# A streaming-window attention and SwiGLU kernel: sink values of one batch loaded by two POOL loads instead of eight SP loads

## The chip, the cores and the metric

The kernel runs on one core of a Trainium2 chip. Five engines of the core appear: TensorE (PE; its weight loads are PEld), VectorE (DVE), ScalarE (ACT), GpSimd (POOL) and SyncE (SP). SP, ACT and POOL each issue DMA transfers to a queue of their own; those that POOL issues change the type of the data on the way (float32 in memory to bfloat16 on the chip) where the destination asks for it. The metric is device time in microseconds (us), the median of several runs; smaller is better.

## What is computed

The inputs are `q`, `k`, `v` of shape (4, 8, 768, 64) (batch, heads, positions, width of a head) and three weight matrices. The reference, cut to what matters:

```
scores = q @ k^T / sqrt(64)
keep   = (key < 4) or (0 <= query - key < 128)     # 4 "sinks" and a window
x      = softmax(scores where keep) @ v            # heads side by side: (3072, 512)
g      = x @ w_gate                                # 512 -> 1536
out    = (g * sigmoid(g) * (x @ w_val)) @ w_out    # 1536 -> 512
```

Every query sees the keys of its window and, besides, the first four keys of its sequence, the sinks. So the values of `v` at positions 0 to 3 of each head are needed by all later queries of the batch.

## The kernel before

**Tiles and stages.** Attention goes by 12 groups of 256 queries, three to a batch. For a group the kernel brings `k` and `q` into transposed form, multiplies them (`step_S`, L271), takes exponentials on ACT, masks them on DVE (L298; group 0: L602), and multiplies with the values `va` (`step_PV`, L332, matmuls in L349). A group that isn't the first of its batch also takes the sinks: `step_K` (L302) makes their scores from `kss`, and `step_sinks` (L322, matmul L329) puts their share into the sum, from a tile `vsb`. The normed result is transposed (`step_X`) into `xT`. The feed-forward part works on blocks of 256 or 512 tokens: `project` (L408, matmuls L414) for gate (`pg`) and value (`pv`), tanh on ACT, two products on DVE, then `down` (L486). A list written by hand weaves the attention steps of later groups into the feed-forward steps of earlier blocks. The order of each engine's instructions is the order in which the program writes them.

**Sink values.** `vcf` holds the sink values of batch 0 in float32: four rows for each head, heads 0 to 3 in partitions 0 to 15, heads 4 to 7 in partitions 32 to 47, a column of ones beside them, the rest zero (DVE memsets, L162 and L163). `load_sinks(vcf, 0, 1)` (L178 to L184) fills it with eight loads of SP, one for each head, 4 rows of 64 values (1 KB) each. POOL then copies partitions 0 to 63 to 64 to 127 (L196). `step_vsb(0)` (L262, called in L632) multiplies `vcf` with a mask of heads `diag_h` on POOL and gives `vsb`, which the sink matmuls of group 1 read. Batches 1 to 3 have `vcl` in place of `vcf`, filled by the same function later (L644).

**The first loads.** SP and ACT bring the first half of the heads of group 0 (`st`, L175) in float32. POOL's instructions then follow in this order: the other half (`x0`, L186), two iotas, the `rows` of group 1 (L100, four loads), the values `va` of groups 0 and 1 (L122, four loads), the first weight tiles `wg` and `wv` (L133), the copy of `vcf` (L196), two small copies into `kss` (L259), two more pairs of weight tiles, `vsb` (L264), then the `nat` tiles of group 2 (L111) and all later loads. The first feed-forward matmuls of TensorE (`gate_held`, L466) need the first `wg` tile. Behind them in TensorE's order stand the sink matmuls of group 1 and the PV matmuls of group 1.

Of the kernel before, what the change touches and what calls it, by code (L numbers as in the profile page):

```python
# [14 lines left out]
def kernel(  # L15
# [12 lines left out]
    nc = tc.nc  # L28
    P = 128
    B, H, S, D = q.shape  # L30
    NS = int(n_sink)
# [63 lines left out]
    def load_rows(g, i):  # L95
        b, c = divmod(g, GC)
        if g not in rows:
            new_rows(g)
        for w in range(2):
            nc.gpsimd.dma_start(  # L100
                rows[g][64 * w:64 * (w + 1), i],
                by_rows((k, q)[i], b, w, ALL, c * 256))

    def load_nat(g):
        b, c = divmod(g, GC)
        x = (natp if g > 3 else rowp).tile(
            [P, 2, 2, DM], BF16, tag="nat" if g > 3 else "rows", name="nat")
        for i, src in ((0, k), (1, q)):
            for j in range(2):
                t0 = c * 256 + j * P  # L110
                nc.gpsimd.dma_start(  # L111
                    x[:, i, j].rearrange("p (h d) -> p h d", d=D),
                    src[b, :, t0:t0 + P].rearrange("h p d -> p h d"))
        nats[g] = x

    def load_v(g):
        b, c = divmod(g, GC)
        va = vpool.tile([P, 2, H, VS], BF16, tag=f"va{g}", name="va")
        nc.vector.memset(va[:, :, :, D:D + 1], 1.0)
        for j in range(2):  # L120
            t0 = c * 256 + j * P
            nc.gpsimd.dma_start(  # L122
                va[:, j, :, 0:D], v[b, :, t0:t0 + P].rearrange("h p d -> p h d"))
        vas[g] = va
# [3 lines left out]
    def load_gate(i, which=(0, 1)):  # L128
        f0, n = sum(FCH[:i]) * P, FCH[i] * P
        both = (wgs, moe_w_gate, "wg"), (wvs, moe_w_val, "wv")  # L130
        for lst, w, nm in (both[x] for x in which):
            t = wpool.tile([P, DMC, n], BF16, tag=f"{nm}{i}", name=nm)
            nc.gpsimd.dma_start(  # L133
                t, w[:, f0:f0 + n].rearrange("(c p) f -> p c f", p=P))
            lst.append(t)
# [12 lines left out]
    vcf = const.tile([P, 1, D + 1], FP32)  # L148
# [29 lines left out]
    def load_sinks(t, b0, b1):  # L178
        for h in range(H):
            r = 32 * (h // 4) + NS * (h % 4)  # L180
            nc.sync.dma_start(
                t[r:r + NS, :, 0:D], v[b0:b1, h, 0:NS].rearrange("b s d -> s b d"))

    load_sinks(vcf, 0, 1)  # L184
    for i in range(2):
        nc.gpsimd.dma_start(x0[:, i, 4:8], by_two((k, q)[i], 4))  # L186
    nc.gpsimd.iota(tq, [[1, P]], base=0, channel_multiplier=0,
# [3 lines left out]
    load_rows(1, 0)  # L191
    load_rows(1, 1)
    load_v(0)
    load_v(1)
    load_gate(0)
    nc.gpsimd.tensor_copy(out=vcf[64:128], in_=vcf[0:64])  # L196

    nc.vector.tensor_scalar(ident, tq, tk, None, op0=ALU.is_equal)
    tq2 = tq.rearrange("p (o x) -> p o x", o=1).broadcast_to([P, 2, P])
# [62 lines left out]
    def step_vsb(b):  # L262
        vsb = const.tile([P, 4, D + 1], BF16, tag=f"vsb{b}", name="vsb")
        (nc.vector if b else nc.gpsimd).tensor_tensor(  # L264
            vsb,
            (vcl[:, b - 1:b] if b else vcf).broadcast_to([P, 4, D + 1]),
            diag_h.rearrange("q (h o) -> q h o", o=1).broadcast_to([P, 4, D + 1]),
            op=ALU.mult)
        vsbs.append(vsb)
# [359 lines left out]
    step_ks(0)  # L629
    load_gate(1)  # L630
    load_gate(2)
    step_vsb(0)  # L632
    load_nat(2)
    load_gate(3)
# [120 lines left out]
```

## Time and profile before

| what | us |
|---|---|
| median of 3 runs | 237.57 (237.53 to 237.66) |
| the profiled execution, its own time | 238.22 |
| its span, first to last instruction | 236.4 |
| TensorE busy in it | 228.7 |
| VectorE busy | 157.5 |
| ScalarE busy | 113.0 |
| POOL busy | 75.3 |

The granted clock of TensorE was 1.00 throughout. The profile is one execution, so its durations are summed against its own 238.22 us; the median of the unprofiled runs is 0.65 us lower.

How to read the lines. In the chain of work that ended last, a line has the start, the duration and what ran. In the timeline a line has the start, the duration, the engine, the line of the program, the operation, its tiles and shapes, and how many such instructions the line takes together. In the waits, a line names who waited for whom, with the total, the number and the longest wait. In the list of DMA issues the last number is the median time from the start of the issue to the landing. In the busy time by stretches a line has the stretch, its length, the busy time of PE, PEld, DVE, ACT and POOL with the number of instructions, the granted clock, the mean share of the DMA engines with packets in flight (over 1 where packets overlap) and the rate in GB/s.

### The profile page before, as it was taken

The page shows a single profiled execution, that of the slowest core. Times are in us where ns is not written, and L with a number is a line of the kernel's source. Part 1 is how long each engine was busy: PE and PEld are TensorE (multiplying, and loading weights), DVE is VectorE, ACT ScalarE, POOL GpSimd, SP SyncE. Part 2 cuts the span into 40 slices and gives each one's busy share as a digit, 9 for nine tenths or more (in the row PEclk, how much of TensorE's full clock was granted, in tenths as well). Part 3 has the DMA queues.
Part 4 walks back from the last instruction along what each step waited for, and adds up shares of the span by engine and source line. Part 5 has one row for each costly group of instructions (what it writes and reads, how often), then busy time and mean ns, then how long its engine had stood idle before and what let it go on. Part 6 is the DMA issues. An engine that isn't in the chain of part 4 may idle for free.

```text
span 236.4 us, 4873 instructions
## 1 busy us (share of the span) xinstructions
PE 228.7 (97%) x1867; PEld 127.7 (54%) x1893; DVE 157.5 (67%) x333; ACT 113.0 (48%) x230; POOL 75.3 (32%) x102
## 2 busy tenths in 40 slices
PE   8979999999999999999999999999999999999994
PEld 5659645795555644544445444444444445488443
DVE  4898888768650988960888980698970598877000
ACT  4784485467453836412836522655622663333221
POOL 8996875723501409204435350080000000000000
PEclk9999999999999999999999999999999999999999
DMA  7999999995998949997979996599314100200132
GB/s 137 156 191 176 182 199 205 159 145 79 153 225 168 134 72 76 129 134 172 144 114 136 132 140 168 133 87 116 67 24 143 58 3 0 44 3 1 47 132 90
DMA packets 108743, 27.62 MB, mean 117 GB/s; under 512 B 95792, under 2 KB 105776, under 8 KB 108720
## 3 DMA queue, kind: packets, MB, share of 16 engines
q0 software_dynamic: 76640, 13.90, 79.2%
q1 hardware_dynamic: 30672, 11.58, 25.2%
q10 hardware_dynamic: 1408, 1.84, 2.8%
q8 instruction: 15, 0.25, 0.4%
q14 instruction: 8, 0.07, 0.1%
HBM read 28.34 MB, written 6.29 MB: 147 GB/s over the span
## 4 chain that ended last, share of the span: by engine, by line
PE 89%; POOL 3%; DMA 3%; issue 1%; ACT 1%; DVE 1%; POOLq 0%; DVEq 0%; ACTq 0%
PE pv L414 26%; PE pd L499 26%; PE pg L414 26%; PE o L349 4%; PE s L286 4%; DMA wg<-in_moe_w_gate_dram 3%; POOL va L122 1%; POOL rows L100 1%; PE o L329 1%; PE pn L239 1%; POOL x L186 1%; ACT th L434 1%; PE pk L314 1%; PE px L393 0%; DVE u L442 0%
## 5 line engine op out<-in xcount | busy, mean ns | idle before, releaser
L442 DVE SCALAR_TENSOR_TENSOR u<-th,pg 128x512 bf16<-128x512 f32 x72 | 49.2, 683 | 39.4 <-ACT th L434 39.4
L414 PE MATMUL pg<-xT,wg 128*128 128x512 bf16 (+1 forms) x353 | 73.4, 336 | 1.9 <-DMA wg<-in_moe_w_gate_dram 1.2
L434 ACT ACTIVATE th<-pg 128x512 f32<-128x512 f32 x72 | 43.4, 603 | 63.1 <-PE pg L414 57.2
L414 PE MATMUL pv<-xT,wv 128*128 128x512 bf16 (+1 forms) x349 | 72.9, 336 | 0.6 <-ACT e L293 0.2
L499 PE MATMUL pd<-wo,ht 128*128 128x512 bf16 (+2 forms) x292 | 64.5, 371 | 0.5 <-issue 0.2
L414 PEld LDWEIGHTS <-wg 128*128 128x128 bf16 x360 | 35.0, 98 | 29.1 <-DMA wg<-in_moe_w_gate_dram 1.5
L453 DVE TENSOR_TENSOR ht<-u,pv 128x512 bf16<-128x512 bf16 x62 | 42.7, 688 | 9.4 <-PE pv L414 2.5
L293 ACT ACTIVATE e<-s 128x512 bf16<-128x512 f32 (+1 forms) x88 | 42.9, 583 | 3.7 <-PE s L286 3.6
L499 PEld LDWEIGHTS <-ht 128*128 128x128 bf16 x300 | 27.9, 98 | 30.3 <-issue 0.3
L414 PEld LDWEIGHTS <-wv 128*128 128x128 bf16 x360 | 32.1, 98 | 20.3 <-issue 1.7
L504 ACT ACTIVATE ot<-pd 128x512 f32<-128x512 f32 (+1 forms) x24 | 14.3, 596 | 46.7 <-PE pd L499 42.7
L111 POOL DMA_DIRECT2D nat<-in_k_dram x20 | 17.7, 890 | 39.5 <-DMA qT<-nat 35.8
L298 DVE TENSOR_TENSOR e<-e,mask 128x1024 bf16<-128x1024 bf16 (+1 forms) x44 | 27.1, 654 | 3.7 <-ACT e L293 3.7
L122 POOL DMA_DIRECT2D va<-in_v_dram x24 | 21.4, 917 | 4.7 <-DMA wo<-in_moe_w_out_dram 2.5
L363 DVE TENSOR_TENSOR xn<-o,rcp 128x256 bf16<-128x256 f32 x45 | 19.1, 424 | 1.5
L349 PEld LDWEIGHTS <-e 128*128 128x128 bf16 x352 | 15.2, 98 | 7.9 <-issue 0.2
L111 POOL DMA_DIRECT2D nat<-in_q_dram x20 | 17.7, 900 | 1.1 <-DMA wg<-in_moe_w_gate_dram 0.5
L349 PE MATMUL o<-va,e 128*128 128x65 bf16 x352 | 17.2, 194 | 0.1
L286 PE MATMUL s<-qT,kT 64*128 64x128 bf16 (+1 forms) x240 | 13.1, 238 | 0.0
L286 PEld LDWEIGHTS <-kT 64*128 64x128 bf16 x240 | 7.7, 94 | 7.4 <-issue 6.4
L506 DVE TENSOR_SCALAR ot<-pd 128x128 f32<-128x128 f32 x1 | 0.3, 292 | 14.3 <-PE pd L499 14.3
L357 DVE RECIPROCAL rcp<-o 128x4 f32<-128x4 f32 x48 | 8.3, 175 | 1.4 <-PE o L349 1.3
(74 smaller groups left out, 91.5 us busy)
## 6 DMA issues: line engine op xcount, KB each, us to landing
out_dram<-ot SPq DMA_DIRECT2D x17, 256.0 KB
va<-in_v_dram POOLq DMA_DIRECT2D x24, 128.0 KB, 6.2
nat<-in_k_dram POOLq DMA_DIRECT2D x20, 128.0 KB, 4.1
nat<-in_q_dram POOLq DMA_DIRECT2D x20, 128.0 KB, 5.5
wg<-in_moe_w_gate_dram POOLq DMA_DIRECT2D x6, 256.0 KB, 7.9
wv<-in_moe_w_val_dram POOLq DMA_DIRECT2D x6, 256.0 KB, 8.2
wo<-in_moe_w_out_dram POOLq DMA_DIRECT2D x4, 384.0 KB, 11.1
out_dram<-ot ACTq DMA_DIRECT2D x6, 256.0 KB
```

What stands on the lines that cost most here:

```text
L111: nc.gpsimd.dma_start(x[:, i, j].rearrange("p (h d) -> p h d", d=D), src[b, :, t0:t0 + P].rearrange("h p d -> p h d"))
L122: nc.gpsimd.dma_start(va[:, j, :, 0:D], v[b, :, t0:t0 + P].rearrange("h p d -> p h d"))
L286: nc.tensor.matmul(pss[2 * pp + h][:, col:col + n], kTs[b][r, p, kk:kk + P], qTs[b][r, p, qq:qq + n], start=True, stop=True)
L293: nc.scalar.activation(e_t[g][:, h0 + h, lo:512], pss[2 * pp + h][:, lo:512], AF.Exp, scale=scale)
L298: nc.vector.tensor_tensor(e, e, m[:, :, lo:512].broadcast_to([P, 2, 512 - lo]), op=ALU.mult)
L349: nc.tensor.matmul(o, l, r, start=(c == 0 and i == 0), stop=(i == len(mms) - 1), skip_group_check=True)
L363: nc.vector.tensor_tensor(xn, po[:, :, 0:D], rcp.broadcast_to([P, 4, D]), op=ALU.mult)
L414: nc.tensor.matmul(ps[:, i * n:(i + 1) * n], ws[fi][:, c, fo * P:(fo + 1) * P], xTs[tb][:, c], start=(c == 0), stop=(c == DMC - 1))
L434: nc.scalar.activation(th, pg, AF.Tanh, scale=0.5)
L442: nc.vector.scalar_tensor_tensor(u, th, 1.0, pg, op0=ALU.add, op1=ALU.mult)
L453: nc.vector.tensor_tensor(hts[tb][:, f:f + 512 // SIZES[tb]].rearrange("p a n -> p (a n)"), u, pv, op=ALU.mult)
L499: nc.tensor.matmul(po, hts[tb][:, f, ts * P:(ts + 1) * P], wos[f // n][:, f % n, lo:hi], start=(f == 0), stop=(f == DFC - 1))
```

## The change

`load_sinks(vcf, 0, 1)` and its eight SP loads are gone. In their place POOL issues two loads, each of 16 rows of 64 values (four heads at once), between the `va` loads of group 0 and those of group 1. `vcf` is float32, so these two loads don't change the type. The copy of `vcf` into its other half, still on POOL, is moved from behind the first weight tiles to just ahead of `step_vsb(0)`, behind the issues of the second and third pairs of weight tiles.

```diff
-    load_sinks(vcf, 0, 1)
     for i in range(2):
         nc.gpsimd.dma_start(x0[:, i, 4:8], by_two((k, q)[i], 4))
...
     load_v(0)
+    for a in range(2):
+        nc.gpsimd.dma_start(vcf[32 * a:32 * a + 4 * NS, 0, 0:D],
+                            v[0, 4 * a:4 * a + 4, 0:NS])
     load_v(1)
     load_gate(0)
-    nc.gpsimd.tensor_copy(out=vcf[64:128], in_=vcf[0:64])
...
     step_ks(0)
     load_gate(1)
     load_gate(2)
+    nc.gpsimd.tensor_copy(out=vcf[64:128], in_=vcf[0:64])
     step_vsb(0)
     load_nat(2)
```

`load_sinks` stays for `vcl`. In the instruction lists POOL has two loads more, SP eight fewer; the instructions of the other engines and their order are the same.

## The prediction

> **What bounds the kernel now.** I read the page first, then the chain that ended last, then the waits of TensorE. TensorE is busy nearly all of the span, so a change counts only where TensorE stands still.
>
> ```profile
> PE 228.7 (97%) x1867; PEld 127.7 (54%) x1893; DVE 157.5 (67%) x333; ACT 113.0 (48%) x230; POOL 75.3 (32%) x102
> ```
>
> The chain says where the start is late: four steps of POOL issuing loads, then the flight of the first gate weights, then dense matmuls.
>
> ```profile
> 1.24 1.65 POOL x L186 x2
> 3.31 2.41 POOL rows L100 x4
> 5.72 3.43 POOL va L122 x4
> 9.16 6.91 DMA wg<-in_moe_w_gate_dram
> 16.11 1.05 PE pg L414 x8
> ```
>
> The waits of TensorE from 14 to 30 us have one row (total, times, longest):
>
> ```profile
> PE pg L414 <- DMA wg<-in_moe_w_gate_dram: 1.2, 1, 1.2
> ```
>
> So TensorE stands idle until 16.11 us for the first `wg` tile, issued by POOL at 9.16. Later waits are short, so a shift of this landing reaches the end nearly whole. The change puts two loads on POOL ahead of that issue. The question is whether the issue or the queue behind it sets the landing.
>
> The DMA issues, asked in stretches (last column: us from issue to landing), answer it: `va` in 7.4 to 8.6, `wg` in 9.1 to 9.5, and a load of `va`'s bytes and row lengths, `nat`, in 55 to 59, where the casting queue (q0) had been empty:
>
> ```profile
> va<-in_v_dram POOLq DMA_DIRECT2D x3, 128.0 KB, 5.4
> ```
>
> ```profile
> wg<-in_moe_w_gate_dram POOLq DMA_DIRECT2D x1, 256.0 KB, 6.9
> ```
>
> ```profile
> nat<-in_k_dram POOLq DMA_DIRECT2D x2, 128.0 KB, 3.8
> ```
>
> With an empty queue 128 KB land after 3.8 us, here after 5.4: each `va` load stands 5.4 - 3.8 = 1.6 us behind earlier bytes. Successive weight tiles land 1.34 us apart (9.16 + 6.9 = 16.06; the next, issued at 9.90 with 7.5, at 17.4). If the second 128 KB of a tile cost half of that, `wg` alone in the queue would take 3.8 + 0.7 = 4.5; it takes 6.9, so 2.4 us are queue.
>
> The busy time by stretches (last two columns: DMA share, GB/s) agrees. From 10 to 12 us POOL issues without a pause. From 22 to 23 POOL is itself stopped, waiting for landings, so there the queue is surely full, and the rate is the same:
>
> ```profile
> 10.00:11.00 1.00, 1.00 (x37) 0.83 (x33) 0.97 (x3) 1.00 (x4) 0.96 (x3) 1.00 2.26 144
> 11.00:12.00 1.00, 1.00 (x33) 0.85 (x29) 0.99 (x5) 0.80 (x2) 0.92 (x4) 1.00 2.43 155
> ...
> 22.00:23.00 1.00, 1.00 (x11) 0.89 (x10) 0.90 (x3) 0.56 (x1) 0.58 (x1) 1.00 2.40 155
> ```
>
> **The change, part by part.**
>
> *Eight SP loads go.* Their issues take 0.276 us each, from 1.8 to 4.9 us. SP's next instruction waits 36.7 us for a POOL memset, so that time is worth nothing. Their packets share the DMA engines with the first POOL loads: SP's queue shows 2.2, 1.7, 2.7 and 0.8% of 16 engines in the four microseconds from 4 to 8, 7.4% or 1.2 engine-us. Spread over 16 engines this is 0.07 us, all on one engine that everyone waits for 1.2 us. The rate before and after their last packet (143 GB/s in 6 to 7, 155 in 7 to 8) hardly moves. Same rows are loaded in both kernels, so I take 0; ends -1.2 and 0.
>
> *Two loads of 16 rows are issued by POOL* at about 7.4, between the second and third `va`. The trace has no such load. `rows` loads (64 x 4 = 256 rows) go 0.61 us start to start, `va` loads (128 x 8 = 1024 rows) 0.875. A straight line through these gives 0.61 - 0.265 x 240/768 = 0.53 for 16 rows. Ends: 0.25 (the shortest SP issue of these sinks) and 0.875. Two cost 1.06, ends 0.5 and 1.75. Third and fourth `va`, `wg` and `wv` are issued that much later. Hidden: 1.06 is under the 1.6 of the `va` loads and the 2.4 of `wg`. At 1.75 the excess over 1.6, 0.15 us, is late; without that cover the 1.06 is late. Taken: 0.
>
> The Trainium skill, "DMA: Bandwidth & Descriptors", "Issuing engine by pattern", speaks against this: it gives simple loads to SP and calls that path generally faster. The rows agree on the issue (0.276 on SP, 0.61 and more on POOL), yet SP's time is free here and POOL's covered; by the rule alone the change would cost POOL's 1.06 us.
>
> *The copy of `vcf` moves* from 10.79 (0.43 to the next start) to behind the four weight issues. `kss` and what follows move by 1.06 - 0.43 = +0.63: `kss` ends at 12.3, and its reader, the `pk` matmuls, start at 13.43. The copy then starts at 14.63 + 0.63 = 15.26. It now waits for the two loads: they stand between the second `va` (6.54 + 5.4 = 11.9) and the third (12.8), so they have landed 2.4 us earlier. Behind the copy on POOL stand `vsb`, the `nat` loads and later weights. `vsb` (0.62) would end at 15.26 + 0.39 + 0.62 = 16.27; its reader is the first sink matmul, at 17.09, in order behind `pg`. Spare: 0.8 us; with the loads at 1.75 in all, 0.1.
>
> The loads behind come 1.06 later. `nat` lands after 8.5 us where 3.8 is the empty queue's time, so 4.7 us of queue cover it. From 18.98 to 23.52 POOL idles 0.20 + 0.58 + 0.64 + 0.94 = 2.4 us for landings, and the delay is gone there.
>
> *DVE beside the moved copy.* `vsb` stood just ahead of four masks of DVE, and the first mask shows it:
>
> ```profile
> 14.63 0.62 POOL L264 TENSOR_TENSOR vsb<-vcf,diag_h 128x260 bf16<-128x260 f32 x1
> ```
>
> ```profile
> 14.90 0.90 DVE L298 TENSOR_TENSOR e<-e,mask 128x1024 bf16<-128x1024 bf16 x1
> ```
>
> ```profile
> 16.92 0.68 DVE L298 TENSOR_TENSOR e<-e,mask 128x1024 bf16<-128x1024 bf16 x1
> ```
>
> Beside `vsb` a mask takes 0.90, alone 0.68: 0.22 us of contention. Now copy and `vsb` both fall inside the masks (14.9 to 17.6, less 0.2). Ends: 0, and a POOL that gets nothing until the last mask ends at 17.4. I take one rest of a mask for each, 2 x 0.22 = 0.44: `vsb` at 16.7, still 0.4 early.
>
> The Trainium skill, "SBUF — State Buffer", "Who interferes with whom", says that a DVE instruction with two SBUF inputs and a GpSimd one that reads SBUF shut each other out, whichever comes first holding on to its end. The 0.90 fits. By the rule each of the two could wait a whole 0.68 mask: an estimate of 16.27 + 1.36 = 17.6, 0.5 us late.
>
> **Sum:** 0 + 0 + 0. Against the profiled execution (238.22 us, span 236.4) that is 238.2; against the median of the runs, 237.57, it is 237.6.
>
> **Rivals.**
> A, all hidden: 237.4 to 237.8. Chance 0.62.
> B, faster: the sinks' packets were on an engine that everyone waits for, and `wg` lands earlier by up to 1.2 us, TensorE's whole wait. For: the landing needs the last engine. Against: the share and the rates above, and `vsb` later. 236.4 to 237.5, likeliest about 237. Chance 0.14, 0.10 of it over 0.2%.
> C, slower: POOL's copy and `vsb` find no gap in DVE's masks. From 17.1 on each microsecond of `vsb` is one of TensorE. Starved to 17.4: 17.4 + 0.39 + 0.62 = 18.4 against 17.1, +1.3: 238.9; half starved, about 238.2. For: 0.90 against 0.68, masks back to back. Against: only one of the two must yield, and the copy beside an earlier mask took 0.39. Chance 0.16, 0.14 over 0.2%.
> D, slower: the 1.6 us are not queue but slower flight under load, so the issue shows in `wg`: +0.5 to +1.1, 238.1 to 238.7. For: 144 GB/s in 10 to 11. Against: the full queue runs no faster. Chance 0.08, 0.07 over 0.2%.
>
> **Numbers.** A measurement of this kernel tells some 0.2% (0.48 us) from no change. Faster 0.10; slower 0.14 + 0.07 = 0.21; same 0.69. The range 237.1 to 238.4 takes in A, the nearer halves of B, C and D, and both ends of the unknown costs except starvation and an empty first queue; about 0.17 is left out.
>
> **What would show it.** Right: `va`'s later loads land after about 4.5 us instead of 5.4, `wg` after 5.9 with its landing still at 16.1, no new wait of TensorE before the sink matmuls at 17.1, and POOL's idle time at 19 to 23 shorter by a microsecond. Wrong: `wg` landing at another time (B earlier, D later), or TensorE waiting for `vsb` after `pg` (C). An issue of over 0.8 us for each small load would upset the sum.

## The result and the profile after

The changed kernel took 238.45 us in the median of 22 runs (237.90 to 241.87), the kernel before beside it 237.51 (22 runs, 237.20 to 239.29). The ratio on record, which leaves out the two slowest runs of the changed kernel and is not that of the medians (1.004), is 1.005, with a 95% interval from 1.0031 to 1.0068: slower by half a per cent. The forecast was no change, 237.6, and the range ended at 238.4.

The profiled execution after took 238.09 us (span 236.3), *less* than the profiled one before (238.22, span 236.4). Compared by these two traces alone the change does nothing, just as forecast. That is the trap of this case: the execution before that was profiled lies 0.7 us above its kernel's median, the one after 0.4 us below.

The chain of the changed kernel (start, duration, what ran) holds the two small loads, and wg's issue has moved from 9.16 to 10.51:

```profile
7.54 1.15 POOL vcf L194 x2
8.69 1.72 POOL va L122 x2
10.51 5.50 DMA wg<-in_moe_w_gate_dram
16.05 1.05 PE pg L415 x8
```

wg's flight, the time from its issue to its landing, is 5.50 us instead of 6.91, so in this pair of traces the delay of 1.35 is swallowed whole. The wait of TensorE is even longer than before, though `wg` lands no later, because TensorE comes to it 0.4 us earlier (its work ahead of the wait ends at 14.48 instead of 14.87):

```profile
PE pg L415 <- DMA wg<-in_moe_w_gate_dram: 1.6, 1, 1.6
```

And in the busy time by stretches (columns as before) the rate falls where before it held at 144, 155, 174 and 197 GB/s from 10 to 14 us:

```profile
10.00:11.00 1.00, 0.98 (x36) 0.84 (x31) 0.96 (x5) 1.00 (x3) 1.00 (x2) 1.00 1.81 133
11.00:12.00 1.00, 1.00 (x29) 0.82 (x23) 0.97 (x3) 0.66 (x3) 1.00 (x3) 1.00 1.85 115
12.00:13.00 1.00, 1.00 (x28) 0.71 (x22) 0.93 (x5) 1.00 (x3) 0.94 (x4) 1.00 1.49 85
13.00:14.00 1.00, 1.00 (x20) 0.61 (x16) 0.97 (x4) 1.00 (x4) 1.00 (x3) 1.00 1.41 142
```

The last two columns say that the queue has run low. From 12 to 13 us the engines still have packets in flight (1.49), but far fewer than the 2.26 and 2.43 of the full queue before, and they move 85 GB/s: `va` and `wg` were issued too late to keep them fed. The cover that the prediction counted on, earlier bytes in the queue behind which the added issue would hide, was used up.

The list of runs shows a second thing. With each run comes the mean granted clock of TensorE. Thirteen of the 22 runs have 0.999 or more, with a median of 238.22; seven have 0.993 (239.5 to 240.0) and two 0.986 (241.5 and 241.9).

### The profile page after: what moved, and what is told of

Its sections match the earlier page's. It is cut to its first block, busy times and chain, and to the rows that moved or that the text cites. A ratio compares the mean times of both kernels' runs of the same rounds, so it can differ in the third digit from the quotient of the medians.

```text
span 236.3 us, 4864 instructions
## 1 busy us (share of the span) xinstructions
PE 228.3 (97%) x1867; PEld 127.0 (54%) x1893; DVE 158.0 (67%) x333; ACT 112.9 (48%) x230; POOL 77.1 (33%) x104
## 4 chain that ended last, share of the span: by engine, by line
PE 89%; POOL 4%; DMA 2%; issue 2%; ACT 1%; DVE 1%; POOLq 0%; DVEq 0%; ACTq 0%
PE pv L415 26%; PE pd L500 26%; PE pg L415 26%; PE o L350 4%; PE s L287 4%; DMA wg<-in_moe_w_gate_dram 2%; POOL va L122 1%; POOL rows L100 1%; PE o L330 1%; PE pn L240 1%; POOL x L185 1%; ACT th L435 1%; PE pk L315 1%; POOL vcf L194 0%; PE px L394 0%
```

## The experiments

Two theories at the start, besides the prediction's rival C (POOL's copy and `vsb` too late). **D:** POOL's added issue holds back `wg`, in every execution. **G:** TensorE, standing still for `wg` (such a wait is called a stand below), has its clock lowered in a part of the executions.

**1. Both kernels again, each with its own profile.** No edit.

> The kernel before, unchanged, so that it has a list of clocks and spans of its own. Theory G (clock): the slower runs of the changed kernel (239.5 to 240, granted clock 0.993, against 238.0 to 238.3 at 1.000) are executions in which TensorE's clock was lowered for a while around its wait for the first wg tile, and the kernel before has few of them: here nearly all runs at clock 1.000 and 237.3 to 237.7. Theory D (issue): the two small loads hold wg back by 0.6 us in every execution; here wg lands before 15.6 us and the span is 235.7 in a typical execution. If the share of runs below clock 1.000 is here as large as in the changed kernel (9 of 22), G falls.

> The changed kernel, unchanged. G: again two groups, about 238.2 at clock 1.000 and about 239.9 at 0.993, about 0.7% of the span apart, some 4 in 10 in the slower one. D alone: one group at 238.1 to 238.3, the others an accident of the first runs.

Measured: 237.60 for the kernel before (11 runs; 237.49 for the other 26 beside it, ratio 1.001, 0.9993 to 1.0026), one of 11 runs at clock 0.993. The changed kernel took 238.21 (8 runs, ratio 1.0038, 1.0022 to 1.0055), one of 8 at 0.993, where G had expected some 4 in 10. The new profile of the kernel before (237.52) is a typical execution, and its chain shows what the first profile hid:

```profile
9.16 6.21 DMA wg<-in_moe_w_gate_dram
15.37 0.05 issue
15.42 0.61 PE pg L414 x4
```

```profile
PE pg L414 <- DMA wg<-in_moe_w_gate_dram: 0.9, 1, 0.9
```

The issue is at 9.16 as in the first profile, the landing 0.70 us earlier, and the execution 0.70 us shorter. In the changed kernel's second profile `wg` is issued at 10.48 and lands 5.6 us later, at 16.1: 0.7 us after the typical one before. D stands. G's share isn't settled by this.

**2. One part alone.** The copy of `vcf` moved, or the SP loads gone with nothing in their place:

```diff
-    nc.gpsimd.tensor_copy(out=vcf[64:128], in_=vcf[0:64])
...
     load_gate(2)
+    nc.gpsimd.tensor_copy(out=vcf[64:128], in_=vcf[0:64])
```

```diff
-    load_sinks(vcf, 0, 1)
```

> The kernel before with only the copy of vcf moved behind the issues of the second and third pairs of weights; the eight SP loads stay. C: carries the slowdown, +0.4 to +0.9 us. G and D: the first wg is issued as before, so 237.4 to 237.6 and clocks at 1.000.

> The kernel before without the eight SP loads: the sink values of batch 0 are left at zero, so that part of the computation is left out, and nothing is put in place. What the removal alone is worth: 237.5 if the SP loads cost nothing, down to 237.2 if they held up the transfers ahead of the first wg (then wg lands earlier than 15.4 us).

Measured: 237.39 (ratio 0.9999, 0.9988 to 1.0011) and 237.51 (0.9995, 0.9980 to 1.0009). Neither part costs or gains anything. B falls: without the SP loads `wg` lands 6.2 us after its issue, as with them. For C this run is not the whole test, since without the two added issues the copy starts 1.3 us earlier (14.17) than in the changed kernel (15.44). The changed kernel's own profiles settle it: there the first sink matmul follows `pg` without a wait, and `vsb` never ends a wait of TensorE.

**3. The POOL loads alone,** added to the kernel before, into a tile that nobody reads; n = 2, 1 and 4:

```diff
     load_v(0)
+    spare = const.tile([P, 1, D], FP32)
+    for a in range(n):
+        nc.gpsimd.dma_start(spare[32 * a:32 * a + 4 * NS, 0, 0:D],
+                            v[0, 4 * (a % 2):4 * (a % 2) + 4, 0:NS])
     load_v(1)
```

> The kernel before, with its eight SP loads and its copy in place, and beside them two more small POOL loads between the va loads, into a tile that nobody reads. Theory D (the 1.2 us of POOL's issue empties the queue, and the first wg lands some 0.65 us later): 238.1 to 238.3, the rate dips below 150 GB/s between 11 and 14 us, wg issued at 10.4 and landed near 16.0. If the slowdown comes of the removal of the SP loads, of the moved copy or of the later sinks: 237.5.

> The same with one more POOL load of 16 rows instead of two. D with some cover: wg is issued 0.6 us later; the two loads cost 0.7 of their 1.3 us, so the queue covers about 0.6, and one alone costs 0 to 0.2: 237.5 to 237.7. If each load costs in proportion (no cover at all): 237.5 + 0.35 = 237.85.

> The kernel before with four more POOL loads of 16 rows between the va loads. D with a cover of 0.6 to 0.7 us: wg is issued 2.5 to 2.6 us later (near 11.7) and lands 5.5 us after that, near 17.2, so 237.5 + 1.9 = 239.4. If the two loads cost 0.65 for another reason than the issue time (a switch of row lengths in the queue, or 16-row transfers as such), four cost twice that, 238.8.

Measured: two loads 238.12 (12 runs, ratio 1.0035, 1.0012 to 1.0058), one load 237.71 (12 runs, 1.0011, 0.9988 to 1.0035), four 240.03 (6 runs, 1.0108, 1.0082 to 1.0134). Two loads alone make the changed kernel's time, with everything else as before: D is shown. The chain of e5 has them ahead of `va` and `wg`, as in the changed kernel:

```profile
7.54 1.18 POOL spare L196 x2
8.72 1.82 POOL va L122 x2
10.54 5.49 DMA wg<-in_moe_w_gate_dram
```

One load can't be told from none. Four loads came out 0.6 us above the expected 239.4, but three of the six runs are at clock 0.993 or less; the three at full clock have 238.91, 239.39 and 240.03. That their median is the expected figure is partly luck: `wg`, issued at 11.60, lands after 4.9 us, earlier than I had put it, and in the profile TensorE also waits 1.0 us for `kss` ahead of `pk`, since the `kss` copies stand behind the loads on POOL. So e9 does not separate the two waits.

What the profiles say of the queue, side by side (each is one execution; landing = issue + flight):

| kernel | wg issued | flight | landed | GB/s, 10 to 14 us | own time |
|---|---|---|---|---|---|
| before, first profile | 9.16 | 6.91 | 16.07 | 168 | 238.22 |
| before (e1) | 9.16 | 6.21 | 15.37 | 169 | 237.52 |
| copy moved (e4) | 9.16 | 5.70 | 14.86 | 169 | 237.29 |
| no SP loads (e8) | 9.17 | 6.16 | 15.33 | 168 | 237.40 |
| one extra (e6) | 9.86 | 5.25 | 15.11 | 159 | 237.27 |
| two extra (e5) | 10.54 | 5.49 | 16.03 | 126 | 239.64 (clock 0.993) |
| after, first profile | 10.51 | 5.50 | 16.01 | 119 | 238.09 |
| after (e2) | 10.48 | 5.61 | 16.09 | 146 | 238.22 |
| after (e13) | 10.54 | 5.50 | 16.04 | 132 | 238.22 |
| four extra (e9) | 11.60 | 4.9 | 16.5 | 95 | 241.28 (clock 0.986) |

With `wg` issued at 9.16 the mean rate is the same 168 or 169 in all four executions, yet the landing differs by 1.2 us. (Experiments 4 and 5 add three more profiles with this issue time: flights of 6.8, 6.6 and 6.0. The median of the seven is 6.2.) Once the issue is 1.3 us later the rate falls to between 119 and 146, and the landing is 16.0 to 16.1 in all four.

The table also says what a landing is worth. Own time minus landing is 222.1 or 222.2 us in every execution at a clock of 0.998 or more but one, before and after. The one is e4, with the earliest landing, at 222.4. So down to a landing near 15.1 the time goes with the landing of `wg`, whatever the kernel, and this alone accounts for the difference. What no run here separates is POOL's time for the two issues from their packets in the queue: none delays POOL without a load. The flights behind the added loads (5.2 to 5.6 us, and 4.9 behind four) are no longer than those without, so the packets show no cost of their own.

**4. The loads behind the first weights,** so that `wg` is issued at 9.2 again:

```diff
-    for a in range(2):
-        nc.gpsimd.dma_start(vcf[32 * a:32 * a + 4 * NS, 0, 0:D],
-                            v[0, 4 * a:4 * a + 4, 0:NS])
     load_v(1)
     load_gate(0)
+    for a in range(2):
+        nc.gpsimd.dma_start(vcf[32 * a:32 * a + 4 * NS, 0, 0:D],
+                            v[0, 4 * a:4 * a + 4, 0:NS])
```

> The changed kernel with the two POOL loads put behind the issues of the first wg and wv tiles. D: wg is issued at 9.16 as before, so 237.3 to 237.6; the copy of vcf and vsb come as late as in the changed kernel. C (copy and vsb late): 238.2 as the changed kernel.

> The changed kernel with the two loads behind the first wg and wv, again, as the other side of the next run on the same chip. The copy of vcf waits for these loads, vsb is late and TensorE stands still twice, 0.9 and 1.7 us. G: 240 to 240.8, most runs at clock 0.993.

Measured: 240.52 (6 runs) and 240.97 (4 runs, ratio 1.0142, 1.0127 to 1.0156). My expectation of 237.3 to 237.6 was wrong, and for a reason that the trace gives at once. POOL's timeline and TensorE's waits of e7:

```profile
10.65 1.24 POOL L196 DMA_DIRECT2D vcf<-in_v_dram  x2
...
17.75 0.23 POOL L633 COPY vcf<-vcf 64x65 f32<-64x65 f32 x1 [2.01 <-DMA vcf<-in_v_dram]
18.07 0.62 POOL L265 TENSOR_TENSOR vsb<-vcf,diag_h 128x260 bf16<-128x260 f32 x1
```

```profile
PE o L330 <- POOL vsb L265: 1.7, 1, 1.7
...
PE pg L415 <- DMA wg<-in_moe_w_gate_dram: 0.9, 1, 0.9
```

4 KB behind 512 KB of weights land 6.6 us after their issue (median of the two; 4.1 and 4.4 in the two profiles of the changed kernel). The copy waits 2.0 us for them, `vsb` comes at 18.7, TensorE stands 1.7 us at the first sink matmul. So `wg` in time isn't enough: the wait is now C's. It doesn't make the whole loss: five of the six runs are also at clock 0.993, and the one at full clock took 239.08.

**5. The clock.** The profile of e5 fell on an execution at 0.993. In its stretches the last three columns are granted clock, DMA share and rate:

```profile
15.00:16.00 1.00, 0.00 (x0) 0.00 (x0) 1.00 (x2) 1.00 (x4) 0.94 (x2) 1.00 1.42 191
16.00:17.00 1.00, 0.93 (x6) 0.75 (x7) 1.00 (x2) 0.48 (x1) 1.00 (x2) 0.70 1.39 186
17.00:18.00 1.00, 1.00 (x10) 0.32 (x8) 0.72 (x2) 0.28 (x1) 1.00 (x2) 0.50 1.41 187
18.00:19.00 1.00, 1.00 (x21) 0.95 (x18) 0.36 (x2) 0.31 (x1) 1.00 (x2) 0.50 1.46 197
19.00:20.00 1.00, 1.00 (x8) 0.73 (x6) 0.76 (x3) 0.00 (x0) 1.00 (x2) 0.59 1.46 198
```

TensorE does nothing from 14.8 to 16.07 (0.00 in the stretch from 15 to 16), and just after it has begun again its clock goes to half. The loss is 0.30 + 0.50 + 0.50 + 0.41 = 1.71 us, a half for 3.4 us. To test the cause I filled the stands of e10's kernel, whose runs are nearly all at 0.993 or less (9 of 10, e7 and e10 together), with matmuls on zeros (their results are overwritten), and the stand of the changed kernel itself, with ten (e3) and with fourteen (e14). The first edit is in `gate_held`, where `project` now runs `fill(10, ps)` ahead of its own matmuls; the second is in `step_sinks`, in e11 alone:

```diff
-        a = gate_a(tb, f)
+        new_h(tb)
+        a = tanh(project(wgs, tb, f, "pg", 10))
...
+                if g == 1 and j == hh == 0:
+                    fill(14, pos[j, hh].rearrange("p h d -> p (h d)"))
```

> The same with matmuls on zeros in both stands of TensorE (ten ahead of the first gate projection, fourteen ahead of the first sink matmul; their results are overwritten). G: the waits stay, the clock isn't lowered, so the runs at 0.993 go and the median falls to about 239.0. If the lowered clock has nothing to do with the stands, the median stays at 240.3 to 240.8.

> The changed kernel with ten more matmuls on zeros in TensorE's wait ahead of the first gate projection, so that TensorE stands still for some 0.5 us less; their result is overwritten. G: the runs at 0.993 go, all runs near 238.2. D or C (POOL's copy and vsb late): no change in the two groups, 238.5 in the median.

> The changed kernel, unchanged, beside the next run on one chip. G: most runs at 238.1 to 238.4 with clock 1.000, a part (between 1 in 8 and 9 in 22, as before) at 239.5 or more with 0.993.

> The changed kernel with fourteen matmuls on zeros in TensorE's wait for the first wg, about 1.6 us of them, as long as the wait; their result is overwritten. G: no run below clock 0.998, all within 238.0 to 238.5; the delay of wg stays, so it isn't faster than 238.0. If runs at 0.993 stay, the stand before wg isn't what lowers the clock in the changed kernel.

Measured: e10 has no run of four above clock 0.993, e11 has all four at 1.000, and the median falls from 240.97 to 239.34, by 1.6 us, one such loss. From 18 to 19 us, e10 and then e11:

```profile
18.00:19.00 1.00, 0.48 (x7) 0.25 (x7) 0.00 (x0) 0.08 (x1) 1.00 (x2) 0.50 1.44 196
```

```profile
18.00:19.00 1.00, 1.00 (x24) 0.67 (x23) 0.06 (x1) 0.00 (x0) 1.00 (x3) 1.00 1.45 196
```

So in this kernel the stands lowered the clock, and busy matmuls, useful or not, kept it. Not every stand does: the first profile before stood for 1.2 us at a clock of 1.00. In the changed kernel the test says less. e13 took 238.41 (12 runs, one at 0.993); e3 (238.59, 7 runs, one of them 240.09 at 0.998) and e14 (238.62, 10 runs) have none below 0.998 but aren't faster, and both lie above what I had expected. In e14's profile the first `pg`, behind the zero matmuls, starts at 16.68, while `wg` had landed at 16.0; in e3's, `wg` landed only at 16.3. In all, the changed kernel unfilled has 11 of 42 runs at 0.993 or less, filled 0 of 17, and the kernel before, where its clocks are listed, 4 of 104. But nine of the eleven are runs of the result; among the runs made beside the filled ones it is 2 of 20 against 0 of 17, which shows nothing. G is shown in e10 and e11; in the changed kernel it fits, and is not shown. Why 9 of the 22 runs of the result fell there and only 2 of the 20 later ones stays open.

**6. A version to beat both?** If the issue of `wg` sets the start, issue it earlier:

```diff
     load_v(0)
-    load_v(1)
     load_gate(0)
+    load_v(1)
```

> The kernel before with the first wg and wv issued ahead of the va loads of group 1 (load_gate(0) before load_v(1)); the sinks as before. If the place in POOL's queue sets when TensorE starts its projections: wg is issued at 7.4 and lands near 14, TensorE's wait of 0.9 us goes, 236.6 to 236.9; va of group 1 then lands near 16 and is read at about 16.5. If it comes later than that, 237.2 or more.

Measured: 237.69 (12 runs, ratio 1.0017, 0.9997 to 1.0038), no gain. `wg`, issued at 7.44, lands 5.7 us later, the wait for it is gone, and the first `pg` starts at 14.90. But DVE's four masks still run to 17.6 (e1: 17.4), and what follows them on DVE can't be earlier. TensorE loses the half microsecond again: 0.3 at the first PV matmuls of group 1 (0.96 us for sixteen, 0.66 in e1), which wait for the second mask until 16.47, and the rest at the next transposes:

```profile
19.12 0.97 PE L393 MATMUL px<-ident,xn 128*128 128x128 bf16 x8
19.93 0.49 PE L414 MATMUL pv<-xT,wv 128*128 128x256 bf16 x3
```

In e1 the same eight transposes take 0.61, and `pv` follows at 19.80. The edit has a side effect that may share in the first loss: the `va` loads of group 1 now stand behind the weights, and the later of them lands near 16.4, about when those PV matmuls go on. e4, where `va` is untouched, agrees: `wg` lands 0.51 us earlier than in e1, and the execution is 0.23 shorter, with the transposes at 0.96. A typical execution before has two chains that end nearly together, the flight of `wg` and DVE's masks. Delaying one costs at once; hastening one gains 0.2 us or so, and then the other is last.

## Why the prediction was wrong

- **What bounds:** right. TensorE's first projection waits for the first `wg`, and a shift of that landing reaches the end (0.70 us of landing, 0.70 us of time between the two profiles of the kernel before).
- **SP's loads at 0:** right (e8).
- **The cost of the issue:** 0.61 us for each load where 0.53 was put; `wg`'s issue moved by 1.35, not 1.06. Mis-sized, but not what failed: with the cover as it was, 1.06 would have been late too.
- **"Hidden: 1.06 is under the 1.6 of the `va` loads and the 2.4 of `wg`":** this is the step that failed. Two sizes in it were wrong. The floor of `wg`'s flight was put at 4.5 us from `nat` on an empty queue; with the queue run low and the issue at 10.5 it is 5.5 to 5.8. And the flight of 6.91 came from an execution in which it was long; over the seven with the issue at 9.2 it goes from 5.70 to 6.91, with a median of 6.2. The cover was 6.91 - 5.5 = 1.4 in the profiled execution, 0.7 in a typical one and 0.2 in the quickest. 1.35 - 0.7 = 0.65 us are late, and the changed kernel's runs at full clock lie 238.22 - 237.51 = 0.71 above the median before. The prediction had noted that the profiled execution was 0.65 us longer than the median, and had not asked where these 0.65 us were. They were in the flight of `wg`, in the very number that the cover was read from. By the same chance a sign that the prediction had named for being right came true, `wg` landing "still at 16.1" (16.0 and 16.1): the typical landing before was 15.4.
- **The equal rate as proof of a full queue:** too weak. The rate is a mean over all engines and several microseconds, and doesn't say when one tile is complete. At the same 168 and 169 GB/s `wg` landed at 14.9, 15.3, 15.4 and 16.1. What made it differ no view here shows.
- **The copy and `vsb`:** right. The copy took 0.45 and `vsb` 0.94 us between the masks (0.39 and 0.62 in the first profile before), `vsb` ended at 16.92, forecast 16.7, still ahead of the sink matmul at 17.03. The masks took 2.95 us together, 2.71 and 2.86 in the two profiles before.

```profile
15.44 0.45 POOL L633 COPY vcf<-vcf 64x65 f32<-64x65 f32 x1
15.98 0.94 POOL L265 TENSOR_TENSOR vsb<-vcf,diag_h 128x260 bf16<-128x260 f32 x1
```

The rule of the Trainium skill that was weighed there ("SBUF — State Buffer", "Who interferes with whom") agrees with these rows in kind: `vsb` took 0.94 us among the masks and 0.62 in e7, where no mask ran beside it. The estimate by that rule, two whole masks, would have meant 17.6.

- **POOL's idle time later:** right; up to the second `va` load of group 2 it is 1.4 us (22.8 to 24.2) where it was 2.4.
- **Rival D,** "+0.5 to +1.1", had the mechanism's place and its size, and a part of its reason. Of the 2.4 us that the prediction called queue, some 1.0 (5.5 less 4.5) stayed in the flight with the queue run low, as D said of all of it; 0.7 was the long execution, and only 0.7 was cover. It was given 0.08.
- **The clock:** not thought of at all. It adds some 0.2 us to the median of the result (238.45 against 238.22) and some 1.6 us to a run at 0.993 (their median is 239.85).

## What to carry to other kernels

Before a margin is read from a profile, compare the profiled execution with the median: if it is longer, the excess sits somewhere, and a margin measured there may be that excess. Here an issue put ahead of the transfer that the busiest engine waits for was charged as soon as the queue ran low, so count such a cover from typical and quick executions, not from one profile. Where two chains end nearly together, lengthening either costs at once and shortening one gains little.

## What the runs showed of the hardware

A stand of TensorE of 1.3 us was enough, in some executions, for its clock to be granted at half for the next 3.4 us (e5); matmuls on zeros in the stands prevented it (e10 against e11). The Trainium skill, "TensorE: Matmul & The Clock Gate", "HAM oscillation — how this bites in real kernels", gives as a rule that TensorE should have no idle gap above some 3.4 us. Here a gap of 1.3 us, well within that rule, was followed by the slow clock in some executions.

A POOL load of 16 rows keeps POOL for 0.61 us in the changed kernel (0.58 in e9), hardly less than one of 256 rows (0.61 start to start): over this range the price is by the load, not by its rows. And its 4 KB take 4.1 and 4.4 us (medians of two) from issue to landing behind two `va` loads, and 5.8 to 6.6 behind two weight tiles (e7, e10, e11): in these runs a small transfer takes the longer, the more stands ahead of it in the queue.
